# Neighbouring rows of the expert weights on one partition, and strided weight reads on TensorE

## The chip, the cores and the metric

The kernel runs on one core of a Trainium2 chip. The metric is the device time of one execution in microseconds. The engines are TensorE (PE, with its weight loads listed apart as PEld), VectorE (DVE), ScalarE (ACT), GpSimd (POOL) and SyncE (SP); 16 DMA engines move data between HBM and SBUF.

## The reference, cut to what matters

Attention with one more term in the softmax's denominator, then a soft mixture of experts over its output:

```python
batch, n_heads, seq, head_dim = (8, 12, 448, 64)
N, D, E, S_per_e, F = (3584, 768, 8, 4, 1024)          # N = 8*448, D = 12*64, 32 slots

scores = scale * q @ k.T
m = max(scores); e = exp(scores - m)
x = (e / (sum(e) + exp(-m) + 1e-9)) @ v                # heads side by side: x is [N, D]

logits = x @ phi                                       # [N, 32]
d = exp(logits - logits.max(0)); d /= d.sum(0) + 1e-9  # over the tokens
slot_input = d.T @ x                                   # [32, D]
for e in range(E):                                     # 4 slots an expert
    h = maximum(slot_input[e] @ w1[e], 0)              # w1 [E, 768, 1024]
    slot_out[e] = h @ w2[e]                            # w2 [E, 1024, 768]
c = exp(logits - logits.max(1)); c /= c.sum(1) + 1e-9  # over the slots
out = c @ slot_out
```

Inputs and output are f32; the kernel works in bf16 with f32 accumulation.

## The kernel before, in words

**Attention.** Work goes by head pairs, 48 of them (`NPAIR`), six to a batch. The order on every engine is written out by hand in one loop over pairs `s`, each with two halves `y`. For a pair, `T` turns q and k on PE (L205) and copies them out (L208 on ACT, L210 on DVE); `A` makes the scores on PE (L227, L237) and takes row maxima on DVE (L231, L240); `W1`, `W2`, `W3` turn the maxima of three pairs (POOL L247, PE L267 and L268, ACT L273); `Bk` makes the turned scores less their maxima on PE (L302, L305) and the exponentials on ACT (L308); `AV` multiplies with v (L339); `N1` copies the result out (L351) and `N2` divides (DVE L360 and L361, POOL L367 to L376), writing the natural-layout `x` of the batch; `PX` turns `x` on PE (L399) into `xT` (ACT L405).

**Slots.** Once a batch, the steps of `P(b)` run in between, at places that the table `post` fixes: logits (`l_mm`, L434), maxima, exponentials `cd` (L474), a rescaling of the running sum `acc` (`corr`, L480), and the slot sums `s_mm` (L489). `s_mm` takes as its stationary operand a 128-token by 128-column block of `x`, as its moving operand 32 columns of `cd`, and accumulates four token blocks into each of 6 column blocks of `ps_s`; four more matmuls with `ones` make the denominators. So `s_mm` has 24 weight loads of `x` and 4 of `ones`. `s_add` adds `ps_s` to `acc` on DVE (L499, L501). For the last batch `s_last` (L506 to L513) makes `siT`, the slots' inputs with D on the partitions, in the block order of `ps_s`.

**Expert weights.** They come in as 16 halves: w1 and w2 of eight experts, cast from f32 to bf16 by the DMA. All these DMAs are issued from POOL by `load_part` (L108), on the one queue that also carries q, k and v (L141, L145, L146). Of the first 11 halves each is loaded in two DMAs (`load_half`, at the steps in `half_at`) into the tile `W`; the other five go, in 15 parts, into the tile `R`, over the buffers of the attention as these come free (`part_at`, and L646, L647, L661, L662). DMAs of one queue are served in their order of issue.

**Experts and output.** `hidden` (L672) multiplies `siT[:, j, :]` with block j of w1, four experts side by side in 32-column strips of PE, and ACT applies relu (L674). `turn` turns `h` by 8 transposes of 128 columns each (L679) into `hT`, and `slots` (L686) multiplies block `kt` of `hT` with block `kt` of w2. At the end `ps_o` (L742) mixes the slot outputs for all tokens, ACT and DVE scale them (L748, L750), and SP issues the output DMAs (L753).

Of the kernel before, what the change touches and what calls it, by code (L numbers as in the profile page):

```python
# [31 lines left out]
def kernel(  # L32
# [10 lines left out]
    nc = tc.nc  # L43
# [6 lines left out]
    KC = DD // 128  # L50
    FK = F // 128
# [16 lines left out]
    ident = const.tile([128, 128], BF16, name="ident")  # L68
# [35 lines left out]

    def load_part(i, z0, z1):
        kind, e = halves[i]
        src = (moe_w1 if kind == "w1" else moe_w2)[e].rearrange("(j p) f -> p j f", p=128)
        gdma(out=w_sb[(kind, e)][:, z0:z1, :], in_=src[:, z0:z1, :])  # L108

    def load_half(i, z, t=None):  # L110

        if t is not None:
            w_view(i, t)
        n = (KC if halves[i][0] == "w1" else FK) // 2
        load_part(i, z * n, (z + 1) * n)
# [6 lines left out]
    with ExitStack() as at:  # L122
# [290 lines left out]
        def P(b):  # L413
            l, new = lb[b % 2], lb[(b + 1) % 2][:, 4, :]
            eng = nc.gpsimd if b < B - 2 else nc.vector
            x = xb[b % 2]
# [65 lines left out]
            def s_mm():  # L482
                ps = pa([128, KC + 1, NS], F32, "ps_s")
                for j in range(KC + 1):
                    for i in range(4):

                        w = x[:, i, j * 128:(j + 1) * 128] if j < KC else \
                            ones[:, int(i == 3):int(i == 3) + 1].to_broadcast([128, 128])
                        nc.tensor.matmul(ps[:, j, :], w, v["cd"][:, 4 + i, :], start=(i == 0), stop=(i == 3))  # L489
                v["ps_s"] = ps  # L490
# [25 lines left out]
            if b < B - 1:  # L516
                return [both(lambda: l_mm(range(KC)), l_ev, c_max), both(l_turn, c_sub), both(s_max, d_sub),
                        both(exps, corr)] + ([c_turn, both(s_mm, s_add)] if late(b) else [both(s_mm, s_add), c_turn])
            return [lambda: l_mm(range(PB - 2)),
                    lambda: l_mm([PB - 2]),  # L520
                    both(lambda: l_mm([PB - 1]), l_ev, l_turn, lambda: keep_busy(2), s_max,
                         d_sub, lambda: exps(4, 8), corr, lambda: keep_busy(5), s_mm, s_last, lambda: keep_busy(2),
                         c_max, c_sub, lambda: exps(0, 4)),
                    c_turn]
# [50 lines left out]
        for s in range(NPAIR + 1):  # L575
            for y in range(2):
# [19 lines left out]
                else:  # L596
                    if 2 <= s < NPAIR - 6:
                        T(s + 6)
                    g = (s + 1) // 3
# [26 lines left out]
            g = (s + 9) // 3  # L626
# [17 lines left out]
            for i, z0, z1 in part_at.get(s, ()):  # L644
                load_part(i, z0, z1)
        load_part(14, 1, 8)  # L646
        load_part(15, 0, 1)  # L647
        nc.vector.reduce_max(fold, ident.rearrange("p (i s) -> p s i", i=4), axis=AX.X)
# [27 lines left out]
        def turn(g):  # L676
            ps = psA.tile([128, FK, 128], BF16, tag="a", name="ps_ht")
            for kt in range(FK):
                nc.tensor.transpose(ps[:, kt, :], h[g][:, kt * 128:(kt + 1) * 128], ident)  # L679
            nc.vector.tensor_copy(hT[g], ps)  # L680

        def slots(g, kts, hfs=range(2)):
# [13 lines left out]
        h = [h0, h1]  # L696
        hT = [wt[:, (1 + g) * F:(2 + g) * F].rearrange("p (k s) -> p k s", k=FK) for g in range(2)]
        slot_out = wt[:, 3 * F + 2 * DD:3 * F + 3 * DD]
        hidden(1, h1, [0])
        turn(0)  # L700
        last[3]()
        hidden(1, h1, [1])
        pss = [pb_("ps_so") for _ in range(2)]
        slots(0, range(4))
        turn(1)

        ps_cs = psA.tile([128, 512], F32, tag="a", name="ps_cs")
# [13 lines left out]
        for half in range(2):  # L721
            hs = slice(half * ND, (half + 1) * ND)
            ps = psA.tile([128, 512], F32, tag="a", name="ps_sel")
# [60 lines left out]
```

## Time and profile before

| | us |
|---|---|
| median of 3 runs (lowest to highest) | 328.88 (327.84 to 330.64) |
| profiled execution, its own time | 327.88 |
| span of the profiled execution | 326.1 |
| PE busy / share of the span | 283.2 / 87% |
| DVE | 252.6 / 77% |
| ACT | 251.5 / 77% |
| POOL | 200.3 / 61% |
| mean granted TensorE clock | 0.952 |
| DMA packets / MB written | 42438 / 54.30 |

The span is the time from the first to the last instruction of the profile; the execution's own time is 1.78 us longer. Matmuls are pipelined and their ends are modelled, so the busy time of PE is more than the time for which it could not have taken further work. The DMAs read f32 and write bf16, so that the bytes read from HBM (85.03 MB) are more than the megabytes that the packets count. The granted clock is 1.00 in the attention and falls only while the outputs are written.

### The profile page before, as it was taken

The page shows a single profiled execution, that of the slowest core. Times are in us where ns is not written, and L with a number is a line of the kernel's source. Part 1 is how long each engine was busy: PE and PEld are TensorE (multiplying, and loading weights), DVE is VectorE, ACT ScalarE, POOL GpSimd, SP SyncE. Part 2 cuts the span into 40 slices and gives each one's busy share as a digit, 9 for nine tenths or more (in the row PEclk, how much of TensorE's full clock was granted, in tenths as well). Part 3 has the DMA queues.
Part 4 walks back from the last instruction along what each step waited for, and adds up shares of the span by engine and source line. Part 5 has one row for each costly group of instructions (what it writes and reads, how often), then busy time and mean ns, then how long its engine had stood idle before and what let it go on. Part 6 is the DMA issues. An engine that isn't in the chain of part 4 may idle for free.

```text
span 326.1 us, 12146 instructions
## 1 busy us (share of the span) xinstructions
PE 283.2 (87%) x5074; PEld 162.6 (50%) x5074; DVE 252.6 (77%) x575; ACT 251.5 (77%) x546; POOL 200.3 (61%) x402
## 2 busy tenths in 40 slices
PE   2898999999999999899999999999899997977800
PEld 1444465565665566556655665565555554541100
DVE  5789999998798979798989889888798364326910
ACT  2466699999898999899898989898899993306800
POOL 8651778779587959595979597958766823000000
PEclk9999999999999999999999999999999999987555
DMA  6990899999999999569999999999536999963997
GB/s 87 139 134 2 123 207 155 200 178 178 173 153 166 176 187 146 83 88 181 145 196 154 198 140 199 147 196 140 84 50 98 148 158 192 199 111 150 441 422 338
DMA packets 42438, 54.30 MB, mean 166 GB/s; under 512 B 2576, under 2 KB 35344, under 8 KB 42000
## 3 DMA queue, kind: packets, MB, share of 16 engines
q0 software_dynamic: 41376, 42.52, 84.1%
q1 hardware_dynamic: 1008, 11.01, 8.0%
q8 instruction: 39, 0.64, 0.8%
q14 instruction: 15, 0.12, 0.1%
HBM read 85.03 MB, written 11.01 MB: 295 GB/s over the span
## 4 chain that ended last, share of the span: by engine, by line
PE 37%; DVE 17%; POOL 16%; DMA 12%; ACT 7%; issue 6%; POOLq 0%; ACTq 0%; DVEq 0%
DVE mx L231 11%; DMA R<-in_k_dram 8%; PE ps_av L339 8%; PE ps_b L302 7%; PE ps_a L227 5%; PE ps_b L305 5%; DMA R<-in_moe_w_dram 4%; PE ps_t L205 4%; POOL R L141 3%; POOL R L367 2%; ACT R L308 2%; PE ps_o L742 2%; POOL R L247 2%; ACT W L748 2%; DVE mx L240 2%
## 5 line engine op out<-in xcount | busy, mean ns | idle before, releaser
L231 DVE TENSOR_REDUCE mx<-ps_a 128x1 f32<-128x448 f32 x288 | 160.2, 613 | 14.0 <-PE ps_a L227 13.6
L308 ACT ACTIVATE R<-ps_b 128x448 bf16<-128x448 f32 x336 | 158.0, 557 | 13.5 <-PE ps_b L305 9.9
L302 PE MATMUL ps_b<-R 64*128 64x448 bf16 (+1 forms) x384 | 82.4, 358 | 1.5 <-ACT R L405 1.2
L305 PE MATMUL ps_b<-mT,sel 64*128 64x448 bf16 (+1 forms) x384 | 79.0, 352 | 0.0
L227 PE MATMUL ps_a<-R 64*128 64x448 bf16 x288 | 68.9, 363 | 5.5 <-DVE mx L231 3.1
L367 POOL TENSOR_TENSOR R<-ubuf,rec 128x384 bf16<-128x384 f32 x44 | 36.3, 825 | 48.1 <-ACT R L405 22.4
L339 PE MATMUL ps_av<-R 128*128 128x65 bf16 (+1 forms) x1536 | 65.0, 196 | 0.4 <-issue 0.2
L339 PEld LDWEIGHTS <-R 128*128 128x128 bf16 (+1 forms) x1536 | 50.3, 100 | 23.7 <-issue 19.5
L205 PEld LDWEIGHTS <-R 64*64 64x64 bf16 x1344 | 31.3, 113 | 19.3 <-issue 6.2
L205 PE MATMUL ps_t<-ident,R 64*64 64x64 bf16 x1344 | 32.1, 197 | 7.5 <-DMA R<-in_q_dram 4.2
L302 PEld LDWEIGHTS <-R 64*128 64x128 bf16 (+1 forms) x384 | 19.6, 96 | 30.3 <-issue 25.6
L305 PEld LDWEIGHTS <-sel 64*128 64x128 bf16 (+1 forms) x384 | 21.4, 97 | 22.2 <-issue 15.0
L405 ACT CAST R<-ps_x 128x512 bf16<-128x512 f32 x47 | 27.8, 591 | 3.4 <-PE ps_x L399 3.1
L240 DVE TENSOR_REDUCE mx<-ps_a 128x1 f32<-128x448 f32 x48 | 29.5, 615 | 0.4 <-PE ps_a L237 0.3
L208 ACT COPY R<-ps_t 128x896 bf16<-128x896 bf16 x20 | 18.3, 915 | 12.4 <-PE ps_t L205 12.4
L351 ACT COPY ubuf<-ps_av 128x455 f32<-128x455 f32 x44 | 25.1, 570 | 1.2 <-PE ps_av L339 1.0
L227 PEld LDWEIGHTS <-R 64*128 64x128 bf16 x288 | 17.8, 94 | 14.4 <-issue 3.6
L376 POOL TENSOR_TENSOR R<-ubuf,rec 128x128 bf16<-128x128 f32 x44 | 17.5, 398 | 3.7
L237 PE MATMUL ps_a<-R 64*64 64x448 bf16 x96 | 18.5, 381 | 0.6 <-DVE mx L231 0.6
L399 PE MATMUL ps_x<-ident,R 128*128 128x128 bf16 x192 | 18.7, 218 | 0.0
L108 POOL DMA_DIRECT2D R<-in_moe_w_dram x15 | 10.7, 714 | 12.7 <-PE ps_s L489 5.3
L247 POOL TENSOR_SCALAR R<-mx 64x6 bf16<-64x6 f32 (+5 forms) x51 | 13.5, 264 | 8.2 <-DVE mx L231 4.7
(126 smaller groups left out, 363.8 us busy)
## 6 DMA issues: line engine op xcount, KB each, us to landing
W<-in_moe_w_dram POOLq DMA_DIRECT2D x22, 768.0 KB, 9.0
out_dram<-W SPq DMA_DIRECT2D x3, 2688.0 KB, 11.2
R<-in_v_dram POOLq DMA_DIRECT2D x32, 192.0 KB, 4.0
R<-in_q_dram POOLq DMA_DIRECT2D x15, 336.0 KB, 6.7
R<-in_k_dram POOLq DMA_DIRECT2D x15, 336.0 KB, 7.7
R<-in_moe_w_dram POOLq DMA_DIRECT2D x3, 768.0 KB, 8.4
out_dram<-W SPq DMA_DIRECT2D x3, 768.0 KB, 4.3
R<-in_moe_w_dram POOLq DMA_DIRECT2D x1, 1344.0 KB, 11.7
```

The source lines that it names most:

```text
L205: nc.tensor.transpose(ps[r, a, c:c + 64], src[r, pl, tok * D:(tok + 1) * D], ident[r, r])
L227: nc.tensor.matmul(pss[hl][:, 0:S], t[r, 0, i * 128:(i + 1) * 128], t[r, 1, :], start=True, stop=True)
L231: nc.vector.reduce_max(mx[g][:, c:c + 1], pss[hl][:, 0:S], axis=AX.X)
L240: nc.vector.reduce_max(mx[g][:, c:c + 1], ps[:, 0:S], axis=AX.X)
L247: neg = lambda o, s: nc.gpsimd.tensor_scalar(o, s, -1.0, None, op0=ALU.mult)
L302: nc.tensor.matmul(outs[hl], t[rs[hl], 1, cols], t[rs[hl], 0, :], start=True, stop=False)
L305: nc.tensor.matmul(outs[hl], sel[rs[hl], 2 * pl + hl:2 * pl + hl + 1].to_broadcast([64, m]), mT[mg(n)][rs[hl], :], start=False, stop=True)
L308: nc.scalar.activation(e, p[:, 0:S], AF.Exp, scale=scale)
L339: nc.tensor.matmul(o, eT[n, i, hl][:, qc], vp[g % 2][:, 2 * pl + hl, i, 0:W65], start=(i == 0 and u == 0 and hl == 0), stop=(i == 3), skip ...
L351: (nc.scalar.copy if on_pool(n) else nc.vector.tensor_copy)(u, src)
L367: eng.tensor_mul(x[:, 0:3, c:c + 128].rearrange("p i (h d) -> p i h d", h=2), u[:, 0:6, 0:D].rearrange("p (i h) d -> p i h d", h=2), rec[: ...
L405: nc.scalar.copy(xT[:, pb, :], pss[0])
```

## The change

In HBM, row r of a weight matrix went to partition `r % 128`, block `r // 128`; now partition `p` holds the rows `p*j_count + j`, so that the rows of one partition are neighbours. For w1 there are 6 blocks, for w2 8. A product over the rows must pair partition and block in the same way on both sides. So the slot sums take, for block j, every sixth column of `x`, starting at j, which puts `siT` in the order of w1's rows; and the transposes of `h` take, for block kt, every eighth column, starting at kt, which puts `hT` in the order of w2's rows. The number and the order of the instructions on each engine are the same in both programs; the DMAs of L108 have one run of elements per partition (for example 128 x 3072) where they had several rows (128 x 3 x 1024).

```diff
     def load_part(i, z0, z1):
         kind, e = halves[i]
-        src = (moe_w1 if kind == "w1" else moe_w2)[e].rearrange("(j p) f -> p j f", p=128)
+        src = (moe_w1 if kind == "w1" else moe_w2)[e].rearrange("(p j) f -> p j f", p=128)
         gdma(out=w_sb[(kind, e)][:, z0:z1, :], in_=src[:, z0:z1, :])
...
                 for j in range(KC + 1):
                     for i in range(4):
 
-                        w = x[:, i, j * 128:(j + 1) * 128] if j < KC else \
+                        w = x[:, i, :].rearrange("p (d j) -> p j d", j=KC)[:, j, :] if j < KC else \
                             ones[:, int(i == 3):int(i == 3) + 1].to_broadcast([128, 128])
                         nc.tensor.matmul(ps[:, j, :], w, v["cd"][:, 4 + i, :], start=(i == 0), stop=(i == 3))
                 v["ps_s"] = ps
...
         def turn(g):
             ps = psA.tile([128, FK, 128], BF16, tag="a", name="ps_ht")
             for kt in range(FK):
-                nc.tensor.transpose(ps[:, kt, :], h[g][:, kt * 128:(kt + 1) * 128], ident)
+                nc.tensor.transpose(ps[:, kt, :], h[g].rearrange("p (d k) -> p k d", k=FK)[:, kt, :], ident)
             nc.vector.tensor_copy(hT[g], ps)
```

## The prediction

> **What bounds the kernel now.** I read the page first, then stretches by engine, then the waits, then the timeline around one of the edited places. In the slices of the page no single engine is full: PE stands at 9 because the modelled ends of its matmuls overlap, and the DMA engines stand at 9 too.
>
> ```profile
> PE   2898999999999999899999999999899997977800
> DVE  5789999998798979798989889888798364326910
> ACT  2466699999898999899898989898899993306800
> DMA  6990899999999999569999999999536999963997
> ...
> q0 software_dynamic: 41376, 42.52, 84.1%
> ```
>
> The second view is the table of stretches. One batch of six head pairs lasts 31.5 us, from one slot sum (`s_mm`, L489) to the next.
>
> ```profile
> 120.45:151.95 31.50, 30.13 (x598) 18.66 (x595) 27.96 (x64) 29.06 (x67) 23.60 (x47) 1.00 0.81 122
> 151.95:183.44 31.49, 30.20 (x598) 18.66 (x595) 28.18 (x64) 28.96 (x67) 25.16 (x49) 1.00 1.08 171
> ```
>
> After the time, the columns are busy PE, PE weight loads, DVE, ACT, POOL, then granted clock (1.00), DMA share, GB/s. ACT works 29 of 31.5 us and DVE 28, so neither has much room to catch up what it once loses, and in the second batch the DMA queue is full (1.08: its packets overlap). The third view is the timeline around one slot sum, PE, then ACT, then DVE.
>
> ```profile
> 120.29 0.75 PE L489 MATMUL ps_s<-cd,R 128*128 128x32 bf16 x24
> 120.89 0.25 PE L489 MATMUL ps_s<-cd,ones 128*128 128x32 bf16 x4
> 120.99 0.38 PE L399 MATMUL ps_x<-ident,R 128*128 128x128 bf16 x4
> ...
> 120.40 0.93 ACT L208 COPY R<-ps_t 128x896 bf16<-128x896 bf16 x1
> 121.41 0.59 ACT L405 CAST R<-ps_x 128x512 bf16<-128x512 f32 x1
> ...
> 121.25 0.39 DVE L499 TENSOR_TENSOR acc<-acc,ps_s 128x224 f32<-128x224 f32 x1 [0.89 <-PE ps_s L489]
> ```
>
> The 24 matmuls whose weights the change re-reads begin 0.60 us before the four with `ones`: 25 ns a load-and-matmul pair. While they run, DVE stands idle for 0.89 us waiting for them, and ACT has just the 0.93 us copy L208; when it ends, the cast L405 starts within 0.08 us, behind the slot sum and the four transposes L399. So PE is what both nearly full engines wait for here, and nothing covers a longer slot sum. The fourth view is PE's waits from 86 to 292 us, where DMA is what ends them.
>
> ```profile
> PE ps_t L205 <- DMA R<-in_k_dram: 2.2, 3, 1.0
> PE ps_so L686 <- DMA R<-in_moe_w_dram: 2.0, 1, 2.0
> ```
>
> Three loads of k come late in the run, and one weight load at the end (PE stands until 291.24, having run dry at 289.27). After that the outputs flow until the span ends.
>
> **The weight loads.** The 16 halves are issued in 37 DMAs (L108), 128 partitions each. Before, a row is a packet: 8 experts x 768 rows of 2048 B for w1 and 8 x 1024 rows of 1536 B for w2, 14336 packets. After, neighbouring rows of a partition lie together in both memories, and the program of the changed kernel has one run per partition in every one of these DMAs, of 1 to 7 rows: 37 x 128 = 4736 packets, 9600 fewer. The packets' records in the trace have medians of 60, 88, 135 and 173 ns for 512, 896, 1536 and 2048 B, a straight line of 22 ns and 0.0736 ns per byte. Three w1 rows in one packet take 22 + 452 = 474 ns instead of 519, four w2 rows also 474 instead of 540, and 9600 x 22 ns over 16 engines are 13 us of engine time, out of 84.1% of 326 = 274. It is estimated from shorter packets; bounds are nothing gained (the runs are cut up again) and this.
>
> What of it is on the path? Only the waits. A w1 half of 384 packets saves 128 x 45 ns / 16 = 0.36 us, a w2 half 0.52. The three late k loads (0.69, 0.49 and 1.04 us of PE standing, at 88, 137 and 232 us) each lie in the one queue behind two halves, so k comes 0.7 to 1.0 us sooner. Bounds for these are 0 and 2.2 us; I take 1.5, since the third has the last half nearly drained before v is issued and ACT then stands next. At the end, the last four DMAs (7, 1, 4 and 3 rows) land between 275.45 and 291.20; by the line they need 8 x (22 x 4 + 113 x 15) ns = 14.3 us instead of 8 x 135 x 15 = 16.2, and the five-row load ahead of them saves 0.7. That is 2.6 us against a wait of 1.97, so the wait goes: **-1.97**, PE being next.
>
> **Issuing them on POOL.** An issue of a half takes 0.82 us for 384 or 512 packets, and the one-row parts 0.55 to 0.63.
>
> ```profile
> L108 POOL DMA_DIRECT2D W<-in_moe_w_dram x22: 760/817/844, 36.4 to 212.4; - x22
> L108 POOL DMA_DIRECT2D R<-in_moe_w_dram x15: 548/761/929, 228.9 to 278.2; - x15
> ```
>
> The long ones come down to that, 0.25 us each, some 8 us of POOL. I cost this at nothing: POOL is busy 25 of 31.5 us and waits 3.4 us for others in each batch, which hides it; if it counted it would be a gain of 0.25 us in one or two places.
>
> **The slot sums.** 8 x 24 loads of 128 x 128 now read every sixth column (12 bytes apart). No row of before shows a strided load on PE. Lower bound: the pair stays at 25 ns, no cost. A middle row is PE's own: the transposes L399 start 55 ns apart, which is a column streamed per clock for 128 columns. An upper one is DVE, the only engine with a far stride to read: the same 128 x 128 `ident` takes 77 ns more across than along.
>
> ```profile
> L648 DVE TENSOR_REDUCE ubuf<-ident 128x32 f32<-128x128 bf16 x1 | 0.4, 356 | 0.0
> L170 DVE TENSOR_REDUCE band<-ident 128x4 bf16<-128x128 bf16 x1 | 0.3, 279 | 0.0
> ```
>
> That would be 25 + 77 = 102 ns a pair. I take 55, since it is the same engine reading the same memory: 24 x 30 ns = 0.72 us a slot sum. All eight lie on the path (the first seven as shown above; the eighth at 277.17 is followed by L506 and the experts), so **+5.8 us**, with bounds of 0 and 24 x 77 ns x 8 = 14.8.
>
> **The turned activations.** 16 transposes (L679) read every eighth column. They already start 55 ns apart, so a load of up to 55 ns stays hidden behind the 128 streamed columns: 0. The upper bound is 16 x (102 - 55) = 0.75 us, on the path in both `turn` calls.
>
> [...]
>
> **The sum.** +5.8 - 1.97 - 1.5 = +2.3 us on a span of 326.1, so 328.4, and 330.2 with the 1.78 us around the span of the profiled execution (327.88). That execution lies 1.0 us below the median of 328.88, so the median to expect is 331.2.
>
> **Rivals.**
> A, strided loads keep pace. Then only the gains are left: -1.97 and -1.5, 325.4; with all of the k waits 324.7. For it: 128 columns are loaded within 25 ns, over twice as fast as they are streamed, so the load has a wide path of its own. Against: that very rate is what neighbouring columns may give.
> B, the memory can't feed a strided load at even a column per clock. Place: the slot sums; price: 4.6 us for every 24 ns that a pair grows over 55. From 61 ns on it outweighs the gains by over 1% (0.192 us x (c - 25) - 3.5 > 3.3). At 80 ns a pair: +10.6, and 0.4 in `turn`, - 3.5: 336.4. At 102 ns: 341. For it: DVE's 77 ns, and DVE and ACT both standing behind PE there. Against: 64 bytes of stride on another engine aren't 12 on this one.
> C, the DMAs don't change: runs cut into the old lengths. Then 328.88 + 5.8 = 334.7. For it: no software packet of before is over 2048 B. Against: the output queue has 21504 B packets at the same rate per byte as its short ones.
>
> **How the numbers follow.** Forecast 0.32, A 0.30, B 0.32, C 0.06. One per cent, 3.3 us, is about what a measurement of this kernel tells from no change (the three runs spread over 2.8). A lies across that border: 0.20 faster, 0.10 same. The forecast's own range, 40 to 62 ns a pair, is 328 to 333: 0.26 same, 0.06 slower. B and C are slower. That makes 0.20 faster, 0.36 same, 0.44 slower. The range goes from A with nearly all gains, 324.5, to B with DVE's price, 341.
>
> **What would show it.** Starts of the L489 matmuls: 55 ns apart right, 25 is A, above 61 is B. DVE's wait for `ps_s` and ACT's at L405 should grow by 0.7 a batch, the batch from 31.5 to 32.2. Packets of the software queue should number some 31800, with 6144 B among them; the issue of a half should take 0.6 us; the wait of L686 for the weights should be gone, and the k waits mostly. L679 should stay at 55 ns. The prediction is wrong if the slot sum grows and the batch doesn't, or if the batch grows without it.

## The result and the profile after

| | before | after |
|---|---|---|
| median of 20 runs each, us (lowest to highest) | 329.27 (326.54 to 334.13) | 331.74 (329.76 to 334.77) |
| ratio, with its 95% interval | | 1.0131 (1.0103 to 1.0159) |
| profiled execution / its span, us | 327.88 / 326.1 | 333.51 / 331.7 |

The ratio compares undisturbed runs alone, while the medians of all runs are only 2.5 us apart. By the ratio the kernel became 1.3% slower, some 4.3 us (3.4 to 5.2). The forecast was 331.2 us, +2.3 on the median then known, with slower as the likeliest sign at 0.44 and a range from 324.5 to 341: sign and range held, the size was about half. That isn't two small errors: the cost came out smaller than forecast, and the gains didn't come at all. The two profiled executions are 5.6 us apart, which is not the price of the change: PE's clock fell to half three times ahead of the outputs in the one after (at 135.51, 190.13 and 282.29 us), and once in the one before (at 291.49); more of this in the last section.

From the page of the changed kernel, the line of the queue that carries the weights:

```profile
q0 software_dynamic: 31776, 42.52, 79.3%
```

9600 packets are gone, as counted, and their recorded time went from 84.1% to 79.3% of 16 engines, that is from 274 to 263 us. Around the second slot sum, PE's timeline of the changed kernel:

```profile
121.86 1.27 PE L489 MATMUL ps_s<-cd,R 128*128 128x32 bf16 x24
122.98 0.25 PE L489 MATMUL ps_s<-cd,ones 128*128 128x32 bf16 x4
123.08 0.38 PE L399 MATMUL ps_x<-ident,R 128*128 128x128 bf16 x4
```

From the first strided pair to the first with `ones` it is now 1.12 us where it was 0.60: 46.5 ns a pair instead of 25. What stands behind it, on ACT's and on DVE's timeline:

```profile
121.98 0.92 ACT L208 COPY R<-ps_t 128x896 bf16<-128x896 bf16 x1
123.50 0.59 ACT L405 CAST R<-ps_x 128x512 bf16<-128x512 f32 x1 [0.60 <-PE ps_x L399]
```
```profile
123.34 0.39 DVE L499 TENSOR_TENSOR acc<-acc,ps_s 128x224 f32<-128x224 f32 x1 [1.40 <-PE ps_s L489]
```

The copy L208 is over 1.04 us after the slot sum's start, as before (122.90, and 121.33 there), but now ACT stands 0.60 us behind it, and DVE's idle time grew from 0.89 to 1.40 us: the 0.52 us passed on in full. PE's waits of the changed kernel from 45 to 300 us, longest first (in all, times, longest):

```profile
PE ps_t L205 <- DMA R<-in_k_dram: 3.0, 3, 1.7
PE ps_m L268 <- POOL R L247: 2.8, 9, 0.3
PE ps_m L267 <- POOL R L247: 1.9, 3, 1.4
```

The wait for the last weights is gone, but in this profile k is waited for longer than before (3.0 us against 2.2), though the halves ahead of it have a third or a quarter of the packets.

### The profile page after: what moved, and what is told of

It reads as the page before. It is cut to its first block, busy times and chain, and to the rows that moved or that the text cites. A ratio compares the mean times of both kernels' runs of the same rounds, so it can differ in the third digit from the quotient of the medians.

```text
span 331.7 us, 12135 instructions
## 1 busy us (share of the span) xinstructions
PE 289.1 (87%) x5072; PEld 167.2 (50%) x5074; DVE 253.5 (76%) x575; ACT 251.3 (76%) x546; POOL 194.2 (59%) x402
## 3 DMA queue, kind: packets, MB, share of 16 engines
q0 software_dynamic: 31776, 42.52, 79.3%
## 4 chain that ended last, share of the span: by engine, by line
PE 48%; POOL 14%; DVE 13%; DMA 8%; ACT 8%; issue 5%; POOLq 0%; ACTq 0%
PE ps_av L339 9%; DVE mx L231 8%; PE ps_b L302 8%; DMA R<-in_k_dram 8%; PE ps_a L227 7%; PE ps_b L305 6%; PE ps_t L205 4%; PE ps_s L489 3%; ACT R L308 3%; ACT W L748 2%; POOL R L367 2%; POOL R L141 2%; PE ps_o L742 2%; PE ps_h L672 2%; PE ps_so L686 2%
## 5 line engine op out<-in xcount | busy, mean ns | idle before, releaser
L205 PEld LDWEIGHTS <-R 64*64 64x64 bf16 x1344 | 31.4, 113 | 19.7 <-issue 5.8
L302 PEld LDWEIGHTS <-R 64*128 64x128 bf16 (+1 forms) x384 | 19.5, 97 | 30.4 <-issue 25.6
L305 PEld LDWEIGHTS <-sel 64*128 64x128 bf16 (+1 forms) x384 | 21.5, 99 | 23.1 <-issue 16.0
L208 ACT COPY R<-ps_t 128x896 bf16<-128x896 bf16 x20 | 18.3, 915 | 13.2 <-PE ps_t L205 13.2
L237 PE MATMUL ps_a<-R 64*64 64x448 bf16 x96 | 18.7, 385 | 0.6 <-DVE mx L231 0.6
L399 PE MATMUL ps_x<-ident,R 128*128 128x128 bf16 x192 | 18.9, 220 | 0.0
L247 POOL TENSOR_SCALAR R<-mx 64x6 bf16<-64x6 f32 (+5 forms) x51 | 13.6, 266 | 8.7 <-DVE mx L231 5.1
L108 POOL DMA_DIRECT2D R<-in_moe_w_dram x15 | 8.4, 564 | 15.9 <-PE ps_s L489 6.2
```

Of the source, the lines that this page charges most:

```text
L205: nc.tensor.transpose(ps[r, a, c:c + 64], src[r, pl, tok * D:(tok + 1) * D], ident[r, r])
L302: nc.tensor.matmul(outs[hl], t[rs[hl], 1, cols], t[rs[hl], 0, :], start=True, stop=False)
L305: nc.tensor.matmul(outs[hl], sel[rs[hl], 2 * pl + hl:2 * pl + hl + 1].to_broadcast([64, m]), mT[mg(n)][rs[hl], :], start=False, stop=True)
L399: nc.tensor.matmul(pss[i // 2 if two else 0][:, o:o + 128], x[:, i, c], ident if i < 3 else ident2, start=True, stop=True)
```

## The experiments

**The two halves of the change apart.** First the loads alone:

```diff
     def load_part(i, z0, z1):
-        ....rearrange("(j p) f -> p j f", p=128)
+        ....rearrange("(p j) f -> p j f", p=128)
```

> Only the weight DMAs take neighbouring rows; the slot sums and the turned activations read contiguous columns as before, so that the products pair other rows and columns than the reference does (same instructions, same sizes). Theory G (the loads gain what was predicted, and the strided reads took it back): 3.5 us faster than before, some 0.989, without the wait for the last weight load, and the late k loads mostly gone. Rival N (the middle of the run gains nothing, because a late k is set by the slowest engine of the queue and not by the weights' bytes): only the end's 2.0 us, perhaps more if PE's clock stays up there, 0.990 to 0.994. Rival O (the long packets cost something of their own in the middle, as the profile after with its k waits of 1.2 and 1.7 us suggests): 0.995 or more.

Measured: 0.9998 (0.9962 to 1.0034), the time over that of the kernel before, with its 95% interval; the other ratios below are of this kind. The loads gain nothing that this measures, so theory G and rival N fall, and rival O gave the number. Its reason is not shown, though. PE's waits of this kernel, 45 to 300 us:

```profile
PE ps_t L205 <- DMA R<-in_k_dram: 3.8, 5, 1.1
PE ps_m L268 <- POOL R L247: 2.7, 9, 0.3
PE ps_m L267 <- POOL R L247: 2.4, 5, 1.3
```

The wait of L686 for the last weights is gone here too, as theory G had it, and yet nothing is gained; the second profile of the kernel before, further down, shows why.

Then the strides alone:

```diff
-                        w = x[:, i, j * 128:(j + 1) * 128] if j < KC else \
+                        w = x[:, i, :].rearrange("p (d j) -> p j d", j=KC)[:, j, :] if j < KC else \
...
-                nc.tensor.transpose(ps[:, kt, :], h[g][:, kt * 128:(kt + 1) * 128], ident)
+                nc.tensor.transpose(ps[:, kt, :], h[g].rearrange("p (d k) -> p k d", k=FK)[:, kt, :], ident)
```

> Only the strided reads; the weight DMAs as before, so that rows and columns are paired otherwise than in the reference. 192 loads at 47 instead of 25 ns are 4.2 us, and 16 at 62 instead of 56 are 0.1. If every slot sum lies on the path: +4.3 us, less some 0.5 that the last slot sum takes out of the wait for the last weights, 1.011 to 1.013. Rival: a longer slot sum is partly caught up in the batch (ACT and DVE have 2.5 to 3.5 us a batch over): 1.005 or less. Rival: it costs more than its own time, because PE's idling makes its clock fall: over 1.015.

Measured: 1.0143 (1.0086 to 1.0200), which holds the 1.0131 of the whole change. So the strided reads make the loss. The interval is 2.8 to 6.6 us for 4.3 us of longer reads: that they cost their own length fits, but neither a part caught up nor a penalty of 2 us is excluded. PE's waits here, from 45 to 300 us:

```profile
PE ps_m L268 <- POOL R L247: 3.0, 10, 0.3
PE ps_t L205 <- DMA R<-in_k_dram: 2.4, 5, 0.9
...
PE ps_so L686 <- DMA R<-in_moe_w_dram: 0.9, 1, 0.9
```

The strides brought no wait of their own, and the one for the last weights is 0.9 us instead of 2.0: PE comes later to it, so that some of the loss is taken out of this wait. The k waits scatter between profiles: 2.2 (before), 2.5 (before, again), 2.4 (here), 2.3 (sweep) and 0.8 us (stride 8) with short packets, 3.0 (the change), 3.8 (loads alone) and 1.2 (thirds) with long ones. That long packets make k later, or earlier, is not shown.

**What a strided load costs.** In the kernel before, each batch's slot sum got a stride of its own:

```diff
+                        sp = (2, 3, 4, 5, 7, 8, 12, 24)[b]
-                        w = x[:, i, j * 128:(j + 1) * 128] if j < KC else \
+                        w = x.rearrange("p i d -> p (i d)")[:, 0:127 * sp + 1:sp] if j < KC else \
```

> The kernel before, with the slot sums of the eight batches reading x at strides of 2, 3, 4, 5, 7, 8, 12 and 24 columns instead of neighbours (each of the 24 loads of a batch reads the same columns of x, so the slots' inputs are others). A measurement of the load by itself. Theory L, 0.49 ns for each 16-byte piece and not under 25 ns: 25, 25, 31, 39, 55, 62, 62, 62 ns a pair. Rival H: 47 ns for strides 2 to 7, whatever they are. Rival: time grows with the bytes spanned: 12 and 24 columns far over 62.

PE's timeline of this kernel around two of the slot sums, with strides of 5 and 8:

```profile
184.77 1.10 PE L490 MATMUL ps_s<-cd,R 128*128 128x32 bf16 x24
185.73 0.25 PE L490 MATMUL ps_s<-cd,ones 128*128 128x32 bf16 x4
...
247.81 1.60 PE L490 MATMUL ps_s<-cd,R 128*128 128x32 bf16 x24
249.26 0.25 PE L490 MATMUL ps_s<-cd,ones 128*128 128x32 bf16 x4
```

The time from the first start to that of the `ones`, over 24, is the cost of a pair: 0.96 / 24 = 40 ns and 1.45 / 24 = 60 ns. All of them, with 1 and 6 from the kernels before and after:

| stride, columns | 1 | 2 | 3 | 4 | 5 | 6 | 7 | 8 | 12 | 24 |
|---|---|---|---|---|---|---|---|---|---|---|
| ns a pair | 25 | 25 | 26.7 | 33 | 40 | 46.5 | 53 | 60.5 | 59.5 | 67 |

From 3 to 8 columns each further column costs 6.7 ns, then it is nearly flat. Rival H falls, and the rival by bytes spanned too. Theory L had the shape right: 128 columns touch 16 more 16-byte pieces with each column of stride, until at 8 columns (16 bytes) each has a piece of its own, and as far the time grows, from 26.7 to 60.5 ns. 6.7 ns for 16 more pieces is 0.42 ns a piece, plus a fixed 6.6 ns, rather than the 0.49 ns without a fixed part that I had put. The sweep shows the times; that the load goes by such pieces is the theory's reading of them. What is left over at 24 columns (6 ns) stays open, and so does whether the bend lies at 16 bytes or at 8 columns, since all the loads are bf16.

**Thirds.** Each half of w1 takes its own rows, three neighbours a partition, so that the stride is 3 and the packets are those of the change (the edit is against the changed kernel; w2's rows stay as there):

```diff
-        src = ...rearrange("(p j) f -> p j f", p=128)            # w1
+        src = moe_w1[e].rearrange("(z p j) f -> p z j f", z=2, p=128)[:, z0 // 3]
...
-                        w = x[:, i, :].rearrange("p (d j) -> p j d", j=KC)[:, j, :] if j < KC else \
+                        w = x[:, i, :].rearrange("p (z d j) -> p z j d", z=2, j=3)[:, j // 3, j % 3, :] if j < KC else \
```

> Each half of w1 keeps its own 384 rows, three neighbouring rows a partition: the same packets of 6144 B as after, while the slot sums read every third column (6 bytes) instead of every sixth; the rest as after, and the reference's product. Theory L (a strided load is paced by the 16-byte pieces of memory it touches: 96 at 12 bytes in 47 ns and 128 at 16 bytes in 62 ns are both 0.49 ns each): 48 pieces take 23.5 ns, so the pairs stay at 25 ns, and the kernel is as fast as with the loads alone. Rival H (anything but neighbouring columns loads at half the rate): 47 ns as after, and the time of after, 1.013.

```profile
120.74 0.78 PE L492 MATMUL ps_s<-cd,R 128*128 128x32 bf16 x24
121.37 0.25 PE L492 MATMUL ps_s<-cd,ones 128*128 128x32 bf16 x4
```

Measured: 0.63 / 24 = 26 ns a pair and 1.0029 (0.9995 to 1.0064). Theory L holds here too, and the loss of the change is gone; but this is the kernel before once more, not a faster one, since the loads have nothing to give.

**A larger dose.** All slot sums of the kernel before at a stride of 8:

```diff
+                        sp = 8
-                        w = x[:, i, j * 128:(j + 1) * 128] if j < KC else \
+                        w = x.rearrange("p i d -> p (i d)")[:, 0:127 * sp + 1:sp] if j < KC else \
```

> The kernel before with all eight slot sums reading x at a stride of 8 columns (the same columns for each block, so other slot inputs), the weight loads as before: a larger dose of the one cost. At 60 ns a pair, as in the sweep, 192 loads cost 35 ns more each, 6.8 us. Theory S (every microsecond of a slot sum is a microsecond of the kernel): 1.0205, against 1.0131 for the 4.3 us of the change. Rival: part of it is caught up in the batch, so that a larger dose costs less than in proportion: 1.015 or less. Rival: the clock falls more often behind longer slot sums: over 1.025.

```profile
121.45 1.60 PE L490 MATMUL ps_s<-cd,R 128*128 128x32 bf16 x24
122.90 0.25 PE L490 MATMUL ps_s<-cd,ones 128*128 128x32 bf16 x4
```

Measured: 59 to 61 ns a pair and 1.0187 (1.0126 to 1.0249), 6.1 us (4.1 to 8.2) for a dose of 6.8. So theory S fits, but the rival that part is caught up isn't excluded: the interval leaves room for two fifths. The profiles speak for some of it. Against the two profiles of the kernel before, the span grew by 2.6 to 2.9 us with the strides alone (4.3 us of longer reads), 0.9 to 1.3 in the sweep (3.9 us) and 3.7 to 4.1 here (6.8 us); and here PE waits 0.8 us for k instead of 2.2, and not at all for the last weights. But each is one execution, and executions of the kernel before differ by 5 us.

**Why the loads gained nothing.** The disputed cost by itself, 28 halves back to back in the old layout and in the new (a half is here half of one weight matrix, one DMA of 768 KB):

```python
for i, (kind, e) in enumerate(halves):        # 8 of w1, 6 of w2
    t = W[:, i * KC * F:(i + 1) * KC * F].rearrange("p (j f) -> p j f", ...)
    src = (moe_w1 if kind == "w1" else moe_w2)[e].rearrange(LAYOUT, p=128)
    m = (KC if kind == "w1" else FK) // 2
    for z in range(2):
        gdma(out=t[:, z * m:(z + 1) * m, :], in_=src[:, z * m:(z + 1) * m, :])
```

> No attention and no products: only 28 of the weight halves (all of w1, six experts of w2) loaded back to back in the old layout, a packet a row, then a few elements of each copied on DVE and written out to fill the output's shape. The disputed cost by itself, to be read beside the next run. Theory P (the prediction's: a packet's recorded time is what it takes of its engine): 16 x 384 packets of 173 ns and 12 x 512 of 135 over 16 engines are 118 us from the first load to the last. Theory V (packets of an engine overlap, so that the 22 ns a packet are latency and not throughput, as shares over 1.00 in the saturated stretches suggest; back to back, w1 halves landed some 3.8 us apart before and after): some 3.75 us a half, 105 us in all.

> The same 28 halves in the new layout, one packet of 6144 B a partition. Theory P: 28 x 128 packets of 474 ns over 16 engines, 106 us, 12 us less than the run before it. Theory V: the same time as the run before it within 2 us. A third way: long packets are slower than short ones in a row, over 108.

The queue of the run with a packet a row, then of the run with long packets, as their DMA answers give it (the loads fill the slices up to 210 GB/s, the outputs the rest):

```profile
GB/s 16 178 210 212 210 211 210 212 211 212 213 212 212 211 210 211 211 212 211 210 209 209 211 209 210 211 210 210 208 211 210 124 402 439 464 402 402 490 414 201
q0 software_dynamic: 12736, 22.02, 87.4%
```
```profile
GB/s 29 187 217 207 220 213 213 220 207 220 215 207 222 213 213 222 206 220 215 207 222 213 213 220 207 220 217 207 220 213 213 133 459 408 408 408 452 465 408 204
q0 software_dynamic: 4032, 22.02, 79.7%
```

The packets' records sum to 119 and 107 us over 16 engines, but from the first packet to the last it took 105.7 and 103.9 us, and halves landed 3.73 and 3.66 us apart on average. Theory V holds: the long packets save 1.8 us of the 12 that theory P gives. With short packets the records overlap by 13 us, with long ones by 3: most of the 12 us that the short packets' records have over the long ones' is such overlap, and not time of the queue. A half gains 0.06 to 0.09 us, where the prediction had 0.36 and 0.52.

**Is a late k worth anything?** POOL's order in the kernel before, one step moved:

```diff
+            if s == 1 or (s and s % 3 == 0):
+                if g < NG:
+                    load(g, "q")
+                    load(g, "k")
             if s % 3 == 0 and g - 2 < NG:
                 V(g - 2)
                 if s and g - 1 < NG:
                     load(g - 1, "v")
-            if s == 1 or (s and s % 3 == 0):
-                if g < NG:
-                    load(g, "q")
-                    load(g, "k")
```

> The kernel before with one step moved in POOL's order: at each third pair q and k are issued ahead of the four copies of v and the two loads of v, the rest as it was. Theory K (a late k is late because 2.9 us of v transfers and 2.1 us of copies stand ahead of it, and what the weights' halves take is not what decides): all k waits of PE after 50 us vanish, 2.2 us of standing and now and then a fall of the clock behind it: 0.991 to 0.995. Rival W (the halves of the weights set it): k waits stay. Rival: v comes late instead, or POOL's copies hold up what follows them: 1.00 or slower.

Measured: 0.9993 (0.9953 to 1.0032). PE's waits of this kernel, 45 to 300 us:

```profile
PE ps_m L268 <- POOL R L247: 3.5, 11, 0.3
PE ps_so L686 <- DMA R<-in_moe_w_dram: 3.1, 2, 2.7
PE ps_m L267 <- POOL R L247: 3.1, 7, 1.0
```

And the last of these in the kernel before:

```profile
PE ps_m L267 <- POOL R L247: 1.3, 5, 0.3
```

No wait for k is left, so theory K is right that the two v loads and the copies ahead of k make it late enough to be waited for; rival W falls. But the time is the same. In this profile PE waits for POOL's `W1` (L247 before L267) 3.1 us instead of 1.3, behind v's copies and loads, which are now later in POOL's order, and 3.1 instead of 2.0 or 2.5 for the last weights. That the gain turned into these waits is a reading of one profile. What is measured is that 2.2 us of k waits less brought between 1.5 us of gain and 1.1 of loss.

**The kernel before, profiled again.**

> The kernel before, profiled once more, to see which of the differences between the profiles are the kernel's: how long PE waits for k and for the last weights, how long from the issue of the seven-row part to the last landing (19.5 us in the first profile, 18.5 after the change, 19.1 and 19.4 with long packets in two experiments), and where the clock falls. If the long packets shorten the end, this is near 19.5 again; if it's chance, anything from 18.5 to 19.5.

It has waits for k of 2.5 us and for the last weights of 2.5, its first four batches take 31.4 to 31.6 us, and it has 20.7 us from the issue of the seven-row part to the last landing. With short packets that stretch was 19.5, 20.7, 18.8 (strides alone), 18.7 (sweep), 19.1 (stride 8) and 20.5 (q and k first); with long ones 18.5 (the change), 19.1 (loads alone) and 19.4 (thirds). The means are half a microsecond apart and the values overlap: a gain of some tenths at the end may be there, 2.6 us are not. In thirds PE still waits 1.13 us for the last weights. With the strides alone and short packets it waits 0.9 us, and at stride 8 not at all. So the missing wait in the profile after is mostly PE's own lateness: its last slot sum takes half a microsecond more, and in that profile its clock was at half from 282.29 to 285.70 us. It is the same with the loads alone, where the wait is gone without a stride: there PE's clock was at half for 6.83 us around its last slot sum (columns: stretch, length, busy PE, PE loads, DVE, ACT, POOL, clock, DMA share, GB/s).

```profile
276.83:283.66 6.83, 6.31 (x59) 3.17 (x59) 2.14 (x8) 1.54 (x5) 0.83 (x2) 0.50 1.00 182
```

## Why the prediction was right or wrong, point by point

**What bounds the kernel: right in the main.** PE's slot sum holds up ACT and DVE. ACT's new idle time of 0.60 us behind L399 and the two doses (1.0143 for 4.3 us, 1.0187 for 6.8) show it, and so does the batch: with the strides alone the first four take 32.0 to 32.5 us instead of 31.4 to 31.5, where 32.2 was forecast. That nothing covers a longer slot sum was too strong: some of it comes out of PE's waits for DMAs (the one for the last weights was 2.0 us before and 0.9 with the strides alone), how much is open.

**The slot sums: mechanism right, the term too large.** I took 55 ns a pair, the distance at which the transposes L399 start, with 128 streamed columns each; it is 46.5, so 192 x 21.5 ns = 4.1 us instead of 5.8. That lies within the 40 to 62 ns of the forecast, so rivals A (25 ns) and B (above 61) fall. The row that I chose has nothing to do with it. Streaming does go by columns and by the clock: the matmuls L388 of 512 columns start 216 ns apart at the full clock and 427 at half (before from 275.63 us on, and the changed kernel from 284.28). But 128 neighbouring columns are loaded in 25 ns and streamed in 55, so that a load doesn't go at the pace of the stream; that a strided one would was my estimate, and the strides of 8, 12 and 24 take longer than that (60.5, 59.5 and 67 ns). In the sweep a strided load's price is 6.7 ns for each column of stride from 3 to 8, or 0.42 ns for each 16-byte piece if theory L is right, and it ends at a stride of 8 columns but for the 6 ns at 24; a stride of 6 costs 21.5 ns. The 25 ns of neighbours are a floor that a stride of 2 doesn't leave (25) and a stride of 3 barely does (26.7).

**The turned activations: nearly right.** They went from 56 to some 62 ns, with the first of each eight at 113 instead of 67: 0.2 us in all, within the bound of 0.75.

**Issuing on POOL: right.** A w1 half's issue takes 0.61 us instead of 0.82 (predicted 0.6), and no time came from it.

**The weight loads: this is the step that failed.** "9600 x 22 ns over 16 engines are 13 us of engine time" took the line through the packets' records as throughput. The line itself was right: the records of 6144 B packets have a median of 474 ns, as forecast. But what they add up to is not the queue's time. I had the counterevidence on the table: a share of 1.08 in a full stretch means that records overlap, and I wrote so, and then summed records all the same. Landings back to back would have told it too: a w1 half of before lands some 3.8 us after the one ahead of it, not 4.15, and the last four DMAs took 15.75 us (275.45 to 291.20) where the line gave 16.2. The runs showed in its place: back to back a half lands 3.73 us after another with short packets and 3.66 with long ones, so 0.06 to 0.09 us are gained on it instead of 0.36 to 0.52. What followed from the step fell with it: -1.97 at the end and -1.5 for the k loads. The lower bound that I gave, nothing gained, was right, but its reason, which is rival C's (runs cut up again), wasn't: the packets became 6144 B.

**The k waits: wrong twice.** Long packets in the halves ahead of it don't bring k sooner by 0.7 to 1.0 us, since a half gains under 0.1; and taking the waits away, by putting k ahead of v, didn't shorten the kernel. Whether the halves ahead have a part in k's lateness is open, since no run took them away.

The terms as measured are 4.1 + 0.2 for the strides and nothing that can be told from zero for the loads (0.9998, give or take 0.4%, or 1.2 us): 4.3 us, inside the 3.4 to 5.2 of the ratio, though above the 2.5 between the medians; the runs don't settle it closer. That the median of 331.74 came within 0.6 us of the forecast 331.2 is luck: a cost put 1.5 us too high made up for part of 3.5 us of gains that didn't come.

## What to carry to other kernels

Before a transfer is credited with fewer packets, look whether its queue is already at its rate. Here the shares were over 1.00 (1.08 from 151.95 to 183.44 us), and halves landed at a steady distance that is shorter than what their records add up to (3.73 us against 119 / 28 = 4.25): the packet records overlapped, and only the distance of landings (3.73 and 3.66 us) priced the change. A strided operand is paid where it is read: 24 short matmuls, 25 ns apart, had hardly any room under which a strided load could hide and came to 46.5 ns, while 16 transposes, 56 ns apart, came to only 62 at a stride of 8, at which the short ones take 60.5. And a wait in the list is worth nothing until an experiment takes it away: PE's k waits went from 2.2 us to zero, other waits grew (1.3 to 3.1 us for POOL, 2.0 to 3.1 for the last weights) and the time stayed (0.9993).

## What the runs showed of the hardware

A 128-column bf16 weight load with a 32-column matmul takes 25 ns up to a stride of 2, some 26.5 at 3, then 6.7 ns more for each column of stride, and 60 at 8; beyond, 59.5 at 12 and 67 at 24. Of the DMA queue: loads that cast from f32 to bf16 run at 210 to 215 GB/s written (768 KB in 3.73 or 3.66 us), whether in packets of 1536, 2048 or 6144 B.

I had not expected PE's clock to fall in the middle of the run; ahead of the prediction I said that it falls only while the outputs are written. PE's stretch of waiting for a late k in the changed kernel, the one after it, and the next (columns: stretch, length, busy PE, PE loads, DVE, ACT, POOL, clock, DMA share, GB/s):

```profile
187.80:189.50 1.70, 0.04 (x3) 0.02 (x2) 0.62 (x2) 0.79 (x2) 0.00 (x0) 1.00 0.99 201
190.13:193.54 3.41, 3.41 (x50) 2.33 (x48) 1.63 (x5) 1.51 (x3) 0.96 (x2) 0.50 0.94 196
193.54:196.95 3.41, 3.41 (x82) 2.32 (x78) 3.06 (x7) 3.40 (x8) 3.21 (x8) 1.00 0.05 11
```

PE stood for 1.7 us, then ran 3.41 us at half clock: 50 matmuls where the next 3.41 us have 82. The profile before has the same 3.41 us behind its wait for the last weights, ahead of the outputs:

```profile
291.49:294.90 3.41, 3.41 (x42) 1.66 (x35) 0.56 (x1) 0.15 (x1) 0.00 (x0) 0.50 0.00 0
```

It isn't sure to happen. PE's wait of 1.54 or 1.55 us ahead of L430 (L433 in thirds) stands in every profile of the whole kernel; the clock fell during it or within 0.8 us of its end in five of them (the change, before again, loads alone, thirds, stride 8) and not in the other four. Waits of 1.16 to 1.18 us (the changed kernel's that ended at 59.6 us, and two in the sweep) passed without. The changed kernel's three stretches at half clock ahead of the outputs lasted 3.41 us each, that of the loads alone 6.83. Why the clock fell behind some waits and not behind others is not settled by these runs, and how much of the spread between runs comes from it was not tried.
